# Where the broadcast of the second mixture's first expert stands in a chained attention and mixture kernel

## The chip, the cores and the metric

The kernel runs on one core of a Trainium2 chip. The metric is the device time of one execution in microseconds. Three executions of the kernel before were timed: 648.74 us median, 644.17 the lowest, 648.91 the highest. A further execution was profiled.

## The reference, cut to what matters

Attention over pooled keys and values feeds a first mixture of experts, whose output feeds a second one. Each token goes to one expert; in the second mixture an expert takes at most `capacity` tokens, in token order.

```
x = attention(q, k, v)                     # 2304 tokens, 512 wide
logits = x @ w_gate + modality_bias[modality_id]
e = argmax(logits);  x[mask e] = gate * relu(x[mask e] @ w1[e]) @ w2[e]     # first mixture, 8 experts, F = 1024
logits = x @ w_gate2
e = argmax(logits);  keep the first `capacity` tokens of each expert
out[kept] = gate * relu(x @ w1[e]) @ w2[e]                                    # second mixture
```

## The kernel before, in words

**Tiles and windows.** A mixture is worked in windows of 256 tokens of one expert (two row tiles of 128). In the first mixture window 0 belongs to the first token's expert and has a hand-written order of its own (`first_window`); windows 1 to 9 run through `mixture.body(w, n)`, with n = 2 for a full window and n = 1 for a half one. Which body runs is decided on the chip: every engine reads a flag from a table and branches (L685), so both bodies of each window stand in the program. In the data used, windows 1 to 7 and window 9 are full, and window 8 is the half one.

**The body of a window.** TensorE (PE) computes the first matrix product in four parts, `first(0)` to `first(3)`, and the second product in four parts from them, `second` and `second_ends`. Each float32 value is split in a high and a low part, so each product is three matmuls (L398, L399, L401 and L438, L439, L440). After each `first`, ScalarE (ACT) writes the high part of the hidden tile, `hh` (L405), and VectorE (DVE) the low part, `hl` (L406). Between them stand the transposes of the next window's tokens (L384, with L387 on ACT and L388 on DVE).

**Work on the window before.** While window w is on PE, an object `post1` treats the output of window w - 1: its 16 products with the second gate's columns run on DVE (L747), in groups of 2, 2, 5 and 7 that stand between the parts of the body. Then `gates` finds each token's second expert, `store` sends the rows to memory from GpSimd (POOL, L790), and at the very end of the window `places` puts the experts into the table `e2acc` with two small matmuls (L798) and one DVE addition (L799).

**The guess.** The second mixture starts with the expert of one token, the first row of window 0 of the first mixture. `guess` (L183 to L194) broadcasts that expert number over the partitions with a matmul (L185) and has DVE write seven things from it: the integer `gi` (L186), the rotated order of the experts `rot`, `wrap` (L188 to L191), the table `before2` (L192), the expert as a column `gs` (L193) and its marker `isgs` (L194). In the kernel before this is the end of `places` for token window 0, which is the end of window 1.

**Who reads it.** `gi` is read by the DMA queue of SyncE (SP), in `loads` (L603), where the second mixture's first weights are asked for; `gs` and `isgs` are read in window 8 (`k2.experts`, `k2.others`), `before2` in the second mixture's dispatch.

**Order.** The schedule is written by hand: each engine works through its instructions in the order of the program, and semaphores hold an instruction until what it reads is there. PSUM tiles named "sums" are taken from a pool of two.

Of the kernel before, what the change touches and what calls it, by code (L numbers as in the profile page):

```python
# [6 lines left out]
F32 = mybir.dt.float32  # L7
# [5 lines left out]
ALU = mybir.AluOpType  # L13
# [56 lines left out]
def build(tc, A, out):  # L70
    nc = tc.nc
    V, G, PE, ACT = nc.vector, nc.gpsimd, nc.tensor, nc.scalar
# [7 lines left out]
    def bc(ap, axis, shape):  # L80
        return ap.unsqueeze(axis).to_broadcast(shape)
# [5 lines left out]
    cp = root.enter_context(tc.tile_pool(name="cp", bufs=1))  # L87
# [6 lines left out]
    def C(name, p=128):  # L94
        o, n = _COLS[name]
        return cb[:p, o : o + n]
# [62 lines left out]
    before2 = cp.tile([128, E, E], F32, name="before2")  # L159
# [23 lines left out]
    def guess(psum_ap, ecol, before, slot):  # L183

        mm(psum_ap, C("sel0"), ecol, start=True, stop=True)  # L185
        V.tensor_copy(gi[0:1, slot : slot + 1], psum_ap[0:1, 0:1])  # L186
        rot = cp.tile([128, E], F32, name=f"rot{slot}")
        V.tensor_scalar(rot, iota[:, 0:E], psum_ap, None, ALU.subtract)  # L188
        wrap = cp.tile([128, E], F32, name=f"wrap{slot}")
        V.tensor_scalar(wrap, rot, 0.0, 8.0, ALU.is_lt, ALU.mult)  # L190
        V.tensor_tensor(rot, rot, wrap, ALU.add)  # L191
        V.tensor_tensor(before, bc(rot, 1, [128, E, E]), bc(rot, 2, [128, E, E]), ALU.is_lt)  # L192
        V.tensor_scalar(gs[slot], psum_ap, float(slot), None, ALU.add)  # L193
        V.tensor_scalar(isgs[slot], rot, 0.0, None, ALU.is_equal)  # L194
# [4 lines left out]
    def bank(use, shape):  # L199
        pool, name = banks[use]  # L200
        return pool.tile(shape, F32, name=name)
# [173 lines left out]
    def scatter(ids, k, y, n):  # L375
        for t in range(n):
            G.indirect_dma_start(  # L377
                out[:, :], bass.IndirectOffsetOnAxis(ap=ids[:, k + t : k + t + 1], axis=0),
                y[:, t, 0:DM], None, bounds_check=N - 1, oob_is_err=False)

    def trans(xg, xT, t):
        px = bank("turned", [128, CH, 128])
        for c in range(CH):
            tp(px[:, c, :], xg[t][:, 128 * c : 128 * c + 128], ident)  # L384
        px = px.rearrange("p c (b r) -> p c b r", b=2)
        hi, lo = (xT[:, :, 2 * t : 2 * t + 2, i, :] for i in range(2))
        ACT.copy(hi, px)  # L387
        V.tensor_tensor(lo, px, hi.bitcast(F32), ALU.subtract)  # L388
# [43 lines left out]
    def second(py, hs, q, order=None):  # L432

        for j, t in order or [(j, t) for j in range(2) for t in range(2)]:
            if t < len(hs):
                hh, hl = hs[t]
                st, sp = (q == 0 and j == 0), (q == NF - 1 and j == 1)
                mm(py[t], hh[:, j, :], h2[q][:, j, :], start=st, stop=False)  # L438
                mm(py[t], hh[:, j, :], l2[q][:, j, :], start=False, stop=False)  # L439
                mm(py[t], hl[:, j, :], h2[q][:, j, :], start=False, stop=sp)  # L440

    def second_ends(py, a2, a3):

        second(py, a2, 2, [(0, 0), (1, 0), (0, 1)])
        second(py, a3, 3, [(0, 0), (1, 0)])
        second(py, a2, 2, [(1, 1)])
        second(py, a3, 3, [(0, 1), (1, 1)])
# [96 lines left out]
    class mixture:  # L544
# [69 lines left out]
        def body(self, w, n):  # L614

            m, xT, y = self.m, self.xT(w), self.y(w)
            first = lambda q: (first2 if n == 1 else first4)(xT, q)
            self.gather(w + 2)
            post = post1(w - 1, self.y(w - 1)) if m == 1 else None
            look, found = (m == 1 and w == WK + i for i in range(2))  # L620
            on_pe = n < 2 or look or found

            def products(n):
                if post and not on_pe:
                    post.products(n)

            py = [psy.tile([128, DM], F32, name=f"py{t}") for t in range(n)]
            if look:
                k2.experts()
            products(2)  # L630
            a0 = first(0)
            if look:
                k2.ranks()
            self.split_late(w - 1, 0)
            self.loads(w, 0)
            self.trans(w + 1, 0)
            products(2)
            a1 = first(1)
            if m == 1 and 2 <= w < 8:
                self.clear_out(w - 2)  # L640
            self.split_late(w - 1, 1)
            self.loads(w, 1)
            self.trans(w + 1, 1)
            if look:
                k2.choose()
            products(5)
            second(py, a0, 0)
            a2 = first(2)
            if post and on_pe:
                post.transposes()  # L650
            if look:
                for f in k2.hot(rt):
                    f()
            products(7)
            second(py, a1, 1)
            if found:
                trans(xgk, xTk, 0)
            if post and on_pe:
                post.logits()
                post.gates()  # L660
            if found:
                trans(xgk, xTk, 1)
            a3 = first(3)
            if look:
                k2.fetch()
            self.split_next(w)
            if post and not on_pe:
                post.gates()
            if post:
                post.store()  # L670
            if look:
                k2.others()
            second_ends(py, a2, a3)
            self.scale(y, py, self.xg(w))
            if m == 2:
                scatter(self.d.ids, self.col(w), y, n)
            elif n == 1:
                ACT.copy(y[:, 1, 0:DM], zero[:, 0:DM])
            if post:
                post.places()  # L680
# [23 lines left out]
        def end(self, w):  # L704

            post = post1(w, self.y(w))
            if w == WK:
                for t in range(2):
                    trans(xgk, xTk, t)

            def transposes():
                post.transposes((ACT.copy, ACT.copy))
                split_hi(rr2, h2, range(3, NF))

            split_hi(rr2, h2, range(1), V.tensor_copy)
            split_hi(rr2, h2, range(1, 3))
            split_lo(rr2, h2, l2, V, range(2))
            k2.hs[0] = first4(xTk, 0, k2.room(0), transposes)
            post.logits()
            post.gates()  # L720

            def places():
                post.places()
                V.tensor_tensor(oh2, bc(e2acc, 2, [128, T2, E]), bc(iota[:, 1 : E + 1], 1, [128, T2, E]), ALU.is_equal)
                k2.rest()
                split_lo(rr2, h2, l2, V, range(2, NF))

            k2.hs[1] = first4(xTk, 1, k2.room(1), places)
            post.store()

    class post1:
# [62 lines left out]
        def places(self):  # L794

            pt = bank("sums", [128, T2])
            for t, (op, oi) in enumerate(self.hot):
                mm(pt, op, oi, start=(t == 0), stop=(t == 1))  # L798
            V.tensor_tensor(e2acc, e2acc, pt, ALU.add)  # L799
            if self.w == 0:  # L800
                e0 = wk.tile([128, 1], F32, name="e0")
                V.tensor_scalar(e0, self.ev[:, 0:1], -1.0, None, ALU.add)
                pg = bank("sums", [128, 1])
                guess(pg, e0, before2, 1)

    e1 = cp.tile([128, T1], F32, name="e1")
    oh1 = cp.tile([128, T1, E], BF16, name="oh1")
    e2acc = cp.tile([128, T2], F32, name="e2acc")  # L810
    tok = cp.tile([128, 2 * W], I32, name="tok")
    fixp = cp.tile([128, 2, NT], F32, name="fix")

# [16 lines left out]
    with ExitStack() as es:  # L830
# [377 lines left out]
        for i in range(T1 + 1):  # L1208
# [25 lines left out]
            if i == 10:  # L1234
                early.close()
                wa = root.enter_context(tc.tile_pool(name="wa", bufs=1, side="right", reuse_waits="tile"))
                wk = root.enter_context(tc.tile_pool(name="wk", bufs=2, side="right", reuse_waits="tile"))
# [111 lines left out]
```

## Time and profile before

| | us |
|---|---|
| median of the three timed executions | 648.74 |
| the profiled execution's own time | 646.96 |
| its span, from the first to the last instruction | 645.2 |
| PE busy in it | 589.3 (91%) |
| DVE busy | 409.8 (64%) |
| ACT busy | 226.3 (35%) |
| POOL busy | 149.5 (23%) |

The busy times are of the whole span, which has several stages: attention up to about 130 us, the first mixture from there to about 380 us, the second after that. What one place in the kernel costs is read from a timeline of that place and from tables of short stretches, not from these shares. PE's matmuls overlap, so the distance between the starts of two of them tells what one costs, not its own length.

### The profile page before, as it was taken

Reading aid. Unit: us, or ns where it says so; the run is one execution under the profiler, and the core shown is the slowest. Engines: PE = TensorE matmul, PEld = TensorE weight load, DVE = VectorE, ACT = ScalarE, POOL = GpSimd, SP = SyncE. Lnnn points to the kernel's source line nnn. Section 1 sums busy time; section 2 is a strip of 40 time slices with the busy share of each in tenths; the row PEclk is TensorE's granted clock in tenths of the full one; section 3 lists DMA queues with packets and bytes.
Section 4 is the critical chain, followed back from the end, with each engine's and each line's share of the span. In section 5 each row is a group of like instructions: output and inputs, shape, how many; then the busy total and the mean of one; then the engine's idle time right before and its main releaser. Section 6 shows DMA issues by size and latency. Waiting matters only on the chain. (4 is left out here: it accounts for less than half of the span.)

```text
span 645.2 us, 11898 instructions
## 1 busy us (share of the span) xinstructions
PE 589.3 (91%) x3990; PEld 529.2 (82%) x3990; DVE 409.8 (64%) x1100; ACT 226.3 (35%) x395; POOL 149.5 (23%) x149
## 2 busy tenths in 40 slices
PE   7768898889999999999899889998899999999990
PEld 4658897879899899989888888997789999988980
DVE  4689789697687686786587586227884571228110
ACT  3433674222122212212244432136673362135210
POOL 1197125021112102202213113122221222122200
PEclk7789999799999999999989979999999999999996
DMA  9999696258133023113207403826886763121100
GB/s 244 246 270 235 210 281 214 67 194 301 54 100 117 37 84 118 47 70 117 64 18 228 148 19 107 289 70 205 274 277 214 258 211 127 52 69 43 52 20 23
DMA packets 57683, 93.12 MB, mean 144 GB/s; under 512 B 6345, under 2 KB 31177, under 8 KB 57412
## 3 DMA queue, kind: packets, MB, share of 16 engines
q1 hardware_dynamic: 47764, 63.97, 32.9%
q0 software_dynamic: 7360, 22.77, 11.0%
q10 hardware_dynamic: 2416, 4.74, 1.9%
q8 instruction: 57, 0.93, 0.6%
q14 instruction: 86, 0.70, 0.4%
HBM read 68.22 MB, written 24.89 MB: 144 GB/s over the span
## 5 line engine op out<-in xcount | busy, mean ns | idle before, releaser
L438 PE MATMUL py<-h,hh 128*128 128x512 f32 x296 | 119.2, 403 | 3.3 <-DVE h L205 1.8
L398 PE MATMUL first<-xT,h 128*128 128x256 f32 x480 | 120.4, 283 | 0.8 <-PE sums L185 0.8
L399 PE MATMUL first<-xT,l 128*128 128x256 f32 x480 | 118.7, 280 | 1.1 <-DVE l L209 1.1
L439 PE MATMUL py<-l,hh 128*128 128x512 f32 x296 | 116.4, 393 | 2.2 <-DVE l L209 2.2
L440 PE MATMUL py<-h,hl 128*128 128x512 f32 x296 | 116.6, 394 | 0.0
L405 ACT ACTIVATE hh<-first 128x512 fp32r<-128x512 f32 x64 | 38.2, 598 | 204.2 <-PE first L401 185.8
L406 DVE SCALAR_TENSOR_TENSOR hl<-first,hh 128x512 fp32r<-128x512 f32 x64 | 44.1, 690 | 99.8 <-ACT hh L405 44.7
L399 PEld LDWEIGHTS first<-xT,l 128*128 128x128 f32 x480 | 90.1, 188 | 3.4 <-DVE l L209 1.9
L398 PEld LDWEIGHTS first<-xT,h 128*128 128x128 f32 x480 | 90.1, 188 | 2.4 <-ACT y L612 0.8
L209 DVE TENSOR_TENSOR l<-rr,h 128x1024 fp32r<-128x1024 f32 x72 | 84.4, 1220 | 4.7 <-ACT h L205 4.4
L747 DVE SCALAR_TENSOR_TENSOR junk<-y,wg2b 128x512 bf16<-128x512 f32 x112 | 77.3, 690 | 3.4
L401 PE MATMUL first<-xT,h 128*128 128x256 f32 x480 | 75.9, 279 | 0.0
L438 PEld LDWEIGHTS py<-h,hh 128*128 128x128 f32 x296 | 55.7, 188 | 14.6 <-ACT hh L428 2.6
L440 PEld LDWEIGHTS py<-h,hl 128*128 128x128 f32 x296 | 55.7, 188 | 13.2 <-DVE hl L413 0.6
L439 PEld LDWEIGHTS py<-l,hh 128*128 128x128 f32 x296 | 55.8, 188 | 13.0 <-DVE l L209 3.1
L401 PEld LDWEIGHTS first<-xT,h 128*128 128x128 f32 x480 | 64.9, 188 | 0.0
L205 ACT CAST h<-rr 128x1024 fp32r<-128x1024 f32 x64 | 63.4, 1043 | 4.2 <-issue 4.2
L377 POOL DMA_INDIRECT out<-y,ids x18 | 24.9, 1384 | 159.7 <-ACT y L612 109.5
L790 POOL DMA_INDIRECT ys<-y,tok x20 | 22.1, 1104 | 168.5 <-DVE y L785 105.6
L1028 PE MATMUL pv<-vaug,eT 96*128 96x146 f32 (+1 forms) x240 | 34.7, 320 | 10.2 <-DVE lgh L1041 10.2
L1028 PEld LDWEIGHTS pv<-vaug,eT 96*128 96x128 f32 (+1 forms) x240 | 31.5, 201 | 12.1 <-issue 7.4
L612 ACT ACTIVATE y<-py,xg 128x512 f32<-128x512 f32 x35 | 24.0, 687 | 38.5 <-PE py L440 28.4
(272 smaller groups left out, 884.2 us busy)
## 6 DMA issues: line engine op xcount, KB each, us to landing
rr<-in_moe_w SPq DMA_DIRECT2D x72, 512.0 KB, 5.4
ys<-zero SPq DMA_DIRECT2D x18, 260.0 KB, 4.5
xs<-xt SPq DMA_DIRECT2D x36, 130.0 KB, 2.7
out<-zero ACTq DMA_DIRECT2D x6, 768.0 KB, 4.4
kin<-in_k SPq DMA_DIRECT2D x3, 1024.0 KB, 8.9
vin<-in_v SPq DMA_DIRECT2D x3, 1024.0 KB, 7.8
qin<-in_q SPq DMA_DIRECT2D x4, 512.0 KB, 14.6
wg2b<-wgd SPq DMA_DIRECT2D x1, 2048.0 KB, 7.3
```

Source lines behind the costliest of these rows:

```text
L205: copy(hi[q], raw[q])
L209: eng.tensor_tensor(lo[q], raw[q], hi[q].bitcast(F32), ALU.subtract)
L398: mm(g[:, j, :], h1[q][:, c, fs], hi, start=(c == 0), stop=False)
L399: mm(g[:, j, :], l1[q][:, c, fs], hi, start=False, stop=False)
L401: mm(g[:, j, :], h1[q][:, c, fs], xT[:, c, :, 1, :], start=False, stop=(c == CH - 1))
L405: ACT.activation(hh, g, AF.Relu)
L406: V.scalar_tensor_tensor(hl, g, 0.0, hh.bitcast(F32), ALU.max, ALU.subtract)
L438: mm(py[t], hh[:, j, :], h2[q][:, j, :], start=st, stop=False)
L439: mm(py[t], hh[:, j, :], l2[q][:, j, :], start=False, stop=False)
L440: mm(py[t], hl[:, j, :], h2[q][:, j, :], start=False, stop=sp)
L747: V.scalar_tensor_tensor(junk, self.y[:, t, 0:DM], 1.0, wg2b[:, e, :], ALU.mult, ALU.mult, accum_out=self.lg[:, t, e : e + 1])
L1028: mm(pv[p0 : p0 + n, j : j + 2, :], eT[:, 3 * half + j, p0 : p0 + n], vaug[b][:, half, j], start=(j == 0), stop=(j == 2), skip_group_check ...
```

## The change

`e20`, the expert number as a column, becomes a tile of its own that stays for the whole kernel, and is still computed by DVE at the end of window 1. The call of `guess` leaves `places` and stands in `body` for window 2, behind `first(0)` and ahead of `split_late`, in both bodies (full and half). Nothing of what `guess` computes is changed, and the number of instructions is the same.

```
             products(2)
             a0 = first(0)
+            if m == 1 and w == 2:
+                guess(bank("sums", [128, 1]), e20, before2, 1)
             if look:
                 k2.ranks()
             self.split_late(w - 1, 0)
...
             V.tensor_tensor(e2acc, e2acc, pt, ALU.add)
             if self.w == 0:
-                e0 = wk.tile([128, 1], F32, name="e0")
-                V.tensor_scalar(e0, self.ev[:, 0:1], -1.0, None, ALU.add)
-                pg = bank("sums", [128, 1])
-                guess(pg, e0, before2, 1)
+                V.tensor_scalar(e20, self.ev[:, 0:1], -1.0, None, ALU.add)
...
     e2acc = cp.tile([128, T2], F32, name="e2acc")
+    e20 = cp.tile([128, 1], F32, name="e20")
```

## Rows read from the trace of the kernel before

**Rows 1.** Table of stretches, windows 1 to 3: length, busy (count) by engine, PEclk.
```profile
151.00:174.70 23.70, 22.52 (x146) 20.05 (x144) 17.98 (x58) 5.16 (x9) 1.42 (x2) 1.00 0.54 190
174.70:198.30 23.60, 23.57 (x154) 21.26 (x155) 17.72 (x55) 4.47 (x8) 3.98 (x4) 1.00 0.22 72
198.30:221.66 23.36, 23.36 (x157) 21.17 (x157) 17.51 (x53) 5.16 (x9) 4.27 (x4) 1.00 0.24 83
```
**Rows 2.** Timeline, PE and DVE, window 1 to 2: start us, length, instruction, idle before.
```profile
172.69 0.39 PE L440 MATMUL py<-h,hl 128*128 128x512 f32 x1
...
172.93 0.21 PE L798 MATMUL sums<-oi,op 128*128 128x18 bf16 x2
...
173.26 0.17 DVE L799 TENSOR_TENSOR e2acc<-e2acc,sums 128x18 f32<-128x18 f32 x1 [2.06 <-PE sums L798]
173.35 0.15 DVE L802 TENSOR_SCALAR e<-ev 128x1 f32<-128x1 f32 x1
...
173.55 0.38 PE L185 MATMUL sums<-e,cb 128*128 128x1 f32 x2 [0.42 <-DVE e L802]
173.97 0.15 DVE L186 CAST gi<-sums 1x1 int32<-1x1 f32 x1 [0.47 <-PE sums L185]
...
174.73 0.35 PE L398 MATMUL first<-xT,h 128*128 128x256 f32 x1 [0.79 <-PE sums L185]
...
174.92 0.16 DVE L194 TENSOR_SCALAR isg<-rot 128x8 f32<-128x8 f32 x1
...
176.13 0.63 DVE L739 TENSOR_SCALAR op<-cb,tkf 128x128 bf16<-128x128 f32 x2 [1.05 <-issue]
```
**Rows 3.** Timeline of PE from window 2 to 3.
```profile
198.01 0.39 PE L440 MATMUL py<-h,hl 128*128 128x512 f32 x1
...
198.25 0.21 PE L798 MATMUL sums<-oi,op 128*128 128x18 bf16 x2
...
198.31 0.37 PE L398 MATMUL first<-xT,h 128*128 128x256 f32 x1
```
**Rows 4.** Timeline of PE where the half window 8 begins.
```profile
316.37 0.72 PE L422 MATMUL first<-xT,h 128*128 128x256 f32 x4 [1.16 <-ACT y L612]
```
**Rows 5.** Timeline of PE in window 2: one group of transposes, the matmul after it.
```profile
177.73 0.60 PE L384 MATMUL turned<-cb,xg 128*128 128x128 f32 x4
...
178.09 0.36 PE L398 MATMUL first<-xT,h 128*128 128x256 f32 x1
```
**Rows 6.** Timeline of DVE in window 2: the four writes of hl.
```profile
178.64 0.69 DVE L406 SCALAR_TENSOR_TENSOR hl<-first,hh 128x512 fp32r<-128x512 f32 x1 [0.62 <-ACTq L577]
...
181.88 0.69 DVE L406 SCALAR_TENSOR_TENSOR hl<-first,hh 128x512 fp32r<-128x512 f32 x1 [0.36 <-ACT hh L405]
...
187.85 0.69 DVE L406 SCALAR_TENSOR_TENSOR hl<-first,hh 128x512 fp32r<-128x512 f32 x1 [0.90 <-ACT hh L405]
...
193.48 0.69 DVE L406 SCALAR_TENSOR_TENSOR hl<-first,hh 128x512 fp32r<-128x512 f32 x1
```
**Rows 7.** Timeline of PE in window 2: the first matmul that reads the last hl.
```profile
195.21 0.40 PE L440 MATMUL py<-h,hl 128*128 128x512 f32 x1
```
**Rows 8.** Timeline of POOL and DVE in window 2: the two gathers, a product beside.
```profile
177.22 0.99 POOL L373 DMA_INDIRECT xg<-xs,rows  x1 [0.51 <-issue]
...
177.32 0.69 DVE L747 SCALAR_TENSOR_TENSOR junk<-y,wg2b 128x512 bf16<-128x512 f32 x1
...
178.51 0.98 POOL L373 DMA_INDIRECT xg<-xs,rows  x1 [0.30 <-DMA ys<-y,tok]
```
**Rows 9.** Timeline in attention: the first mixture's own guess, POOL beside it.
```profile
62.01 2.37 POOL L892 TENSOR_TENSOR tree<-vin 128x1024 f32<-128x1024 f32 x1 [2.10 <-DMA vin<-in_v]
...
62.15 2.26 DVE L194 TENSOR_SCALAR isg<-rot 128x8 f32<-128x8 f32 x1
```
**Rows 10.** SP's queue, line 603: its read of gi (count, ns, start us).
```profile
L603 SPq TENSOR_LOAD <-gi x1: 267/267/267, 216.5 to 216.5; - x1
```
**Rows 11.** Waits of SP's queue: who for whom, us in total, times, longest.
```profile
SPq L106 <- DVE l L209: 120.3, 1, 120.3
```

More of the change, by code (lines that the diff above doesn't have):

```diff
@@ L631, in body @@
             a0 = first(0)
+            if m == 1 and w == 2:
+                guess(bank("sums", [128, 1]), e20, before2, 1)
             if look:
@@ L800, in places @@
             if self.w == 0:
[L801 to L804, printed above, removed]
+                V.tensor_scalar(e20, self.ev[:, 0:1], -1.0, None, ALU.add)
     e1 = cp.tile([128, T1], F32, name="e1")
@@ L810, in build @@
     e2acc = cp.tile([128, T2], F32, name="e2acc")
+    e20 = cp.tile([128, 1], F32, name="e20")
     tok = cp.tile([128, 2 * W], I32, name="tok")
```

## The prediction

> **What bounds the kernel.** I read the table of stretches first, window by window through the first mixture, to learn which engine sets the pace there. In window 3 PE is busy for all of its 23.36 us and DVE for 17.51 [rows 1]; windows 4 to 7 repeat that within 0.1 us. So a full window lasts as long as PE's matmuls, and an idle stretch of PE around it is paid in full. Windows 1 and 2 are the two that are longer, 23.70 and 23.60 us [rows 1]. [...]
>
> Second, I read the timeline of PE and DVE across the border of windows 1 and 2 [rows 2]. The reader is to see a chain that passes from engine to engine: the last matmul of the window starts at 172.69, the two of `places` at 172.93, DVE adds them at 173.26, then computes the expert number at 173.35, and only then can PE do the broadcast, at 173.55, after 0.42 us of idling for it. The next window's first matmul starts at 174.73, with 0.79 us idle before it. From the last L440 to that L398 it is 174.73 - 172.69 = 2.04 us. Third, the same distance at the next border: 198.31 - 198.01 = 0.30 us [rows 3]. The borders of windows 3 to 4, 4 to 5, 5 to 6, 6 to 7 and 8 to 9 show 0.30 as well, so six in all; only the entry into the half window 8 is longer.
>
> The page's chain that ended last is of no help here: it follows the second mixture's scatters and never comes to this place.
>
> **The change part by part.**
>
> *The broadcast leaves the border.* If window 1 then ends like the other full ones, the border goes from 2.04 to 0.30: 1.74 us won on PE. The 0.42 us are surely tied to the broadcast, which waits for DVE. The 0.79 us behind it need a reading: the row puts them down to the broadcast itself [rows 2], though that had ended at 173.93, and no data that `first(0)` reads was late. I take it that PE's queue runs ahead over the branch while matmuls are still at work, and can't when its next matmul waits for DVE. At the other six borders, which have the same branch and no such wait, L398 follows L798 by 0.06 us [rows 3]. So I count the 0.79 as won too. The bounds are 1.74 - 0.79 = 0.95 and, if window 2's surplus over window 3 also goes (23.60 - 23.36 = 0.24 [rows 1]), 1.74 + 0.24 = 1.98 us.
>
> *The broadcast enters window 2 on PE.* Two matmuls with their weight loads, between `first(0)` and the transposes. Four transposes, as short as these, take 178.09 - 177.73 = 0.36 us from their start to the next one's [rows 5], 0.09 each, so two take 0.18; the broadcast's own 0.38 us for both [rows 2] is the upper end, if nothing overlaps. I take 0.23, near the transposes, which load weights of the same 128 columns and move more data. Its wait is free: in the new place PE comes to it 177.73 - 174.73 = 3.0 us after the window's first matmul [rows 2, 5], about 176.0, and `e20` is written at about 173.5 (173.35 + 0.15 [rows 2]). Its PSUM tile is free too, since the addition that last read one ends at 173.43.
>
> *The seven DVE instructions enter window 2.* From 173.97 to 174.92 + 0.16 = 175.08 they take 1.11 us [rows 2]. At the border they lay beside PE's idling; DVE's next work, L739, started 1.05 us after them. Now they stand behind the first write of `hl` and ahead of the low half of the transposed tokens (L388). Queued behind them on DVE are that L388, two products, and the second `hl`. DVE idles for 0.36 us ahead of the second `hl` and 0.90 us ahead of the third, both times for ACT, which waits for PE [rows 6]: 1.26 us, more than 1.11. So the third `hl` is written when it was, and the fourth, ahead of which DVE doesn't idle, as well. If this cover were gone, the next to feel it would be the fourth `hl`: it ends at 193.48 + 0.69 = 194.17 [rows 6] and the matmul that first reads it starts at 195.21 [rows 7], 1.04 us to spare. The second `hl`, up to 0.75 us late, is read only after `first(2)`, several us on. I cost this at nothing; the bounds are 0 and 1.11 us.
>
> *e20 instead of e0, gi later.* One DVE instruction as before, in the same place: nothing. `gi` comes some 4 us later than at 174.1. SP's queue is the one that reads it, at 216.5 [rows 10], and behind that it stands for 120.3 us, until DVE has used up the old weights [rows 11]. The other readers come in window 8. Nothing is late; POOL has no instruction in the guess, and its stores and gathers are issued in the same order.
>
> *Sum.* 1.74 - 0.23 = 1.51 us less. Against the profiled execution's own 646.96 that is 645.45. That execution lies 1.78 under the median of the three timed, from which the sum gives 647.23. As 644.17 to 648.91 is shown for one kernel, neither anchor is better; I put the time midway, at 646.3. A move of 1% either way (6.5 us) is about what a measurement of this kernel can tell from no change, and every case here lies within it.
>
> **The rivals.**
>
> *The branch keeps its price.* The 0.79 us could belong to the branch into window 2 and not to the broadcast. For it: the entry into the half window shows 1.16 us of idling where no data was awaited that another border lacks [rows 4]. Against it: six borders without such a pause, with the same branch to the full body. Gain 0.95 - 0.23 = 0.72: 646.2 by the profiled execution, 648.0 by the median. [...]
>
> *The gain is given back.* Something later that doesn't move with PE would take up the 1.5 us, and the time stays at 647.0 (648.7 by the median). For it: the page's chain runs through DMA and issue. Against it: the only large load of weights that is asked for ahead of its turn is held by DVE's use of the old ones [rows 11], so it moves with the windows.
>
> *DVE is held by POOL, and slower.* The same marker instruction L194 took 2.26 us in attention, where POOL's addition ran from 62.01 to 64.38 beside it [rows 9], against 0.16 at the border. In its new place the guess falls on POOL's gathers, 0.99 and 0.98 us long [rows 8]. If DVE's work there grows by more than 1.26 + 1.04 = 2.30 us, PE waits at the fourth `hl`; from 2.30 + 1.51 = 3.81 us on, the change is slower than before. Two instructions held like that one would make 1.11 + 2 x 2.10 = 5.31, so a stall of 3.0 and 1.5 us more than before: 648.5, or 650.2 by the median. Against it: the gathers are shorter than that addition, and a product that runs beside one takes its usual 0.69 [rows 8]; even held for both gathers, 1.11 + 1.97 = 3.08, the change would still gain 0.7. [...]
>
> **How the numbers follow.** The forecast, a gain between 1.2 and 1.9 us, gets 0.78; the branch that keeps its price 0.09; the gain given back 0.09; slower by DVE 0.04. All four lie within 3.0 us of each other, less than the 4.7 us between the timed executions, so the range is made of that spread: from 644.17 less 1.5, 642.7, to 648.91, which is where the gain given back would still put the highest, so 649.0. Faster by over 1% would need under 642.3: 0.04, for a lucky set of executions. Slower by over 1%: 0.02. Within: 0.94.
>
> **What would show it.** Right: from the last L440 of window 1 to the first L398 of window 2 some 0.3 us; L185 in window 2 with no idling before it; seven DVE instructions of together 1.1 us behind the first `hl`; the idle times of 0.36 and 0.90 us ahead of the second and third `hl` smaller or gone; the fourth `hl` over 1 us ahead of its reader; window 2 about 0.2 us longer on PE, and all later borders 1.5 us earlier. Wrong: a pause of 0.8 us that stays at the border; L194 or its neighbours over 1 us beside a gather; PE idling in window 2; or a later wait of PE grown by what the border lost.

## The result, and the profile after

The changed kernel takes 652.57 us (median of 20 executions), the kernel before 648.12 beside it: a ratio of 1.0097, with a 95% interval of 1.007 to 1.0124. The ratio is taken over fast executions alone (one of the changed kernel's 20 is left out) and is not the quotient of the two medians, which is 1.0069. It is slower, where a gain of 1.5 us was forecast, and 652.57 lies above the forecast's range of 642.7 to 649.0. The profiled execution took 648.68 us with a span of 646.9.

At the place of the change the trace shows what was forecast. First the timeline of PE and DVE from window 1 to 2, which answers to [rows 2].

```profile
173.24 0.39 PE L440 MATMUL py<-h,hl 128*128 128x512 f32 x1
173.48 0.21 PE L800 MATMUL sums<-oi,op 128*128 128x18 bf16 x2
173.54 0.36 PE L398 MATMUL first<-xT,h 128*128 128x256 f32 x1
...
173.91 0.15 DVE L803 TENSOR_SCALAR e<-ev 128x1 f32<-128x1 f32 x1
...
176.50 0.28 PE L185 MATMUL sums<-e,cb 128*128 128x1 f32 x2
...
176.64 0.63 PE L384 MATMUL turned<-cb,xg 128*128 128x128 f32 x4
```

The border takes 173.54 - 173.24 = 0.30 us, not 2.04, and the broadcast waits for nothing: `e20` is written 2.4 us ahead of it. Then DVE and POOL in window 2, and PE's first read of the last `hl` (they answer to [rows 6 to 8]).

```profile
177.52 0.69 DVE L406 SCALAR_TENSOR_TENSOR hl<-first,hh 128x512 fp32r<-128x512 f32 x1
177.99 0.99 POOL L373 DMA_INDIRECT xg<-xs,rows  x1 [0.33 <-issue]
178.13 0.14 DVE L186 CAST gi<-sums 1x1 int32<-1x1 f32 x1
...
178.44 0.17 DVE L190 TENSOR_SCALAR wrap<-rot 128x8 f32<-128x8 f32 x1
...
179.06 0.16 DVE L194 TENSOR_SCALAR isg<-rot 128x8 f32<-128x8 f32 x1
...
181.32 0.68 DVE L406 SCALAR_TENSOR_TENSOR hl<-first,hh 128x512 fp32r<-128x512 f32 x1
...
186.93 0.69 DVE L406 SCALAR_TENSOR_TENSOR hl<-first,hh 128x512 fp32r<-128x512 f32 x1 [0.54 <-ACT hh L405]
...
192.58 0.69 DVE L406 SCALAR_TENSOR_TENSOR hl<-first,hh 128x512 fp32r<-128x512 f32 x1
...
194.32 0.40 PE L440 MATMUL py<-h,hl 128*128 128x512 f32 x1
```

The seven instructions run from 178.13 to 179.22, 1.09 us, beside a gather (177.99 to 178.98), and none is stretched: 0.14 to 0.23 us each, 0.15 to 0.22 before. L194, which took 2.26 us beside POOL's addition in attention, takes 0.16 here, but starts 0.08 us after the gather's end; L190, an instruction of the same kind and size, runs inside it and takes its usual 0.17 us. DVE's idle times ahead of the second and third `hl` shrink from 0.36 and 0.90 to 0 and 0.54, and the fourth `hl` ends at 193.27, still 1.05 us ahead of its reader. SP reads `gi` at 217.0, and its longest wait is the same (120.6 us, for L209).

The loss is in windows that hold nothing of the change. The table of stretches for windows 2 to 4 (columns as in [rows 1]):

```profile
173.54:197.42 23.88, 23.88 (x160) 21.52 (x159) 18.35 (x61) 5.17 (x9) 4.21 (x5) 1.00 0.26 82
197.42:221.11 23.69, 23.69 (x157) 21.32 (x157) 17.57 (x53) 5.17 (x9) 4.28 (x4) 1.00 0.26 82
221.11:244.81 23.70, 23.70 (x158) 21.33 (x157) 17.57 (x53) 5.17 (x9) 4.36 (x4) 1.00 0.24 80
```

Window 3 takes 23.69 us and not 23.36, and windows 4 to 6 take 23.70. PE has no idle time in them, as many instructions (157 or 158 in a stretch) and the same granted clock of 1.00: it does the same work in 1.4% more time. The page's costliest groups say which work; first the kernel before, then the changed one (count, busy us, mean ns of one).

```profile
L398 PE MATMUL first<-xT,h 128*128 128x256 f32 x480 | 120.4, 283 | 0.8 <-PE sums L185 0.8
L399 PE MATMUL first<-xT,l 128*128 128x256 f32 x480 | 118.7, 280 | 1.1 <-DVE l L209 1.1
L439 PE MATMUL py<-l,hh 128*128 128x512 f32 x296 | 116.4, 393 | 2.2 <-DVE l L209 2.2
```

```profile
L398 PE MATMUL first<-xT,h 128*128 128x256 f32 x480 | 121.9, 286 | 0.0
L399 PE MATMUL first<-xT,l 128*128 128x256 f32 x480 | 120.2, 282 | 1.2 <-DVE l L209 1.2
L439 PE MATMUL py<-l,hh 128*128 128x512 f32 x296 | 117.3, 396 | 2.2 <-DVE l L209 2.2
```

These matmuls are 2 to 3 ns longer in the mean. Their steps tell it better, that is the distance between the starts of two neighbours, averaged over windows 3 to 6: in the first product (367 distances) 119.26 ns before and 121.31 after, in the second (176) 229.48 and 233.03. (The first product's means hold seven distances of some 200 ns, each the first behind other work; without them they are 117.64 and 119.73, and this 117.64 is the 117.7 of two expectations below.) Over the kernel's 3 x 480 matmuls of the first and 3 x 296 of the second that makes 1440 x 2.05 + 888 x 3.55 = 6.1 us. That takes windows 3 to 6 for the whole kernel and is too much: averaged over the whole kernel, distances over 180 and 300 ns left out, the steps go from 117.68 to 119.44 and from 230.61 to 233.03, which makes 1440 x 1.76 + 888 x 2.42 = 4.7 us.

What has changed for these matmuls is where their operands lie. The built programs give their SBUF tiles addresses from both ends: the "left side" from the low addresses upwards (an added tile of 4 bytes puts `xT0` 32 bytes up, e1 below), the "right side" from the high ones downwards (a tile added there puts `h1_0` 32 bytes down, e4). In the allocation of both programs, all tiles stand at multiples of 32 bytes; `e20` moves every later tile on the left side by 32 bytes, and the absence of `e0` moves `hh` and `hl` by 64. In bytes, modulo 128 in brackets: `h1_0` 184224 (32) in both; `xT0` 104416 (96) before, 104448 (0) after; `hh` 172000 (96) and 172064 (32); `h2_0` 59168 (32) and 59200 (64).

### The profile page after: what moved, and what is told of

Read it like the earlier page. It is cut to its first block, busy times and chain, and to the rows that moved or that the text cites. A ratio compares the mean times of both kernels' runs of the same rounds, so it can differ in the third digit from the quotient of the medians.

```text
span 646.9 us, 11898 instructions
## 1 busy us (share of the span) xinstructions
PE 594.1 (92%) x3990; PEld 530.2 (82%) x3990; DVE 411.9 (64%) x1100; ACT 226.7 (35%) x395; POOL 149.1 (23%) x149
## 5 line engine op out<-in xcount | busy, mean ns | idle before, releaser
L398 PE MATMUL first<-xT,h 128*128 128x256 f32 x480 | 121.9, 286 | 0.0
L399 PE MATMUL first<-xT,l 128*128 128x256 f32 x480 | 120.2, 282 | 1.2 <-DVE l L209 1.2
L440 PE MATMUL py<-h,hl 128*128 128x512 f32 x296 | 116.9, 395 | 0.0
L209 DVE TENSOR_TENSOR l<-rr,h 128x1024 fp32r<-128x1024 f32 x72 | 84.4, 1221 | 4.6 <-ACT h L205 4.4
L401 PE MATMUL first<-xT,h 128*128 128x256 f32 x480 | 77.0, 282 | 0.0
L440 PEld LDWEIGHTS py<-h,hl 128*128 128x128 f32 x296 | 55.5, 187 | 13.8 <-DVE hl L413 0.8
L1028 PE MATMUL pv<-vaug,eT 96*128 96x146 f32 (+1 forms) x240 | 33.1, 307 | 10.9 <-DVE lgh L1041 10.9
L1028 PEld LDWEIGHTS pv<-vaug,eT 96*128 96x128 f32 (+1 forms) x240 | 29.8, 191 | 12.7 <-issue 6.3
```

The source lines that it names most:

```text
L209: eng.tensor_tensor(lo[q], raw[q], hi[q].bitcast(F32), ALU.subtract)
L398: mm(g[:, j, :], h1[q][:, c, fs], hi, start=(c == 0), stop=False)
L399: mm(g[:, j, :], l1[q][:, c, fs], hi, start=False, stop=False)
L401: mm(g[:, j, :], h1[q][:, c, fs], xT[:, c, :, 1, :], start=False, stop=(c == CH - 1))
L1028: mm(pv[p0 : p0 + n, j : j + 2, :], eT[:, 3 * half + j, p0 : p0 + n], vaug[b][:, half, j], start=(j == 0), stop=(j == 2), skip_group_check ...
```

## The experiments

**Theory:** the addresses lengthen PE's steps, wherever the guess stands. **Rival:** the moved code does. The table has the operands' places modulo 128 (of the first product h1 and xT, of the second hh and h2), the steps in ns, the length of window 3 in us, the measured ratio with its interval, and a ratio by estimate. The estimate takes each step's difference to the kernel before, times 1440 and 888, and 0.8 us less where the guess is moved (from e2, below), over 648. As it goes by windows 3 to 6, it tends to be high: with the steps of the whole kernel the change comes to 1.006, e1 and e4 to 1.008.

| run | guess | h1, xT | first | hh, h2 | second | window 3 | ratio | estimate |
|---|---|---|---|---|---|---|---|---|
| before | old | 32, 96 | 119.26 | 96, 32 | 229.48 | 23.36 | | |
| after | moved | 32, 0 | 121.31 | 32, 64 | 233.03 | 23.69 | 1.0097 (1.007 to 1.0124) | 1.008 |
| e5, the same again | moved | 32, 0 | 121.31 | 32, 64 | 233.03 | 23.70 | 1.0068 (1.0032 to 1.0105) | 1.008 |
| e1 pad only | old | 32, 0 | 121.25 | 96, 64 | 233.68 | 23.71 | 1.0052 (1.0026 to 1.0078) | 1.010 |
| e2 move only | moved | 32, 96 | 119.27 | 96, 32 | 229.49 | 23.35 | 0.9986 (0.9958 to 1.0014) | 0.999 |
| e14, e2 again | moved | 32, 96 | 119.26 | 96, 32 | 229.48 | 23.35 | 0.9981 (0.9952 to 1.0009) | 0.999 |
| e3 after, 64 bytes | moved | 32, 32 | 120.10 | 32, 96 | 231.66 | 23.56 | 1.0018 (0.9984 to 1.0052) | 1.004 |
| e4 right pad | old | 0, 96 | 121.29 | 64, 32 | 233.59 | 23.73 | 1.0072 (1.0045 to 1.01) | 1.010 |
| e6 after, right pad | moved | 0, 0 | 120.08 | 0, 64 | 232.49 | 23.58 | 1.0036 (0.9996 to 1.0075) | 1.005 |
| e7 xT alone | old | 32, 0 | 121.27 | 96, 32 | 229.52 | 23.52 | 1.0067 (1.0029 to 1.0106) | 1.004 |
| e8 hh alone | old | 32, 96 | 119.40 | 64, 32 | 233.24 | 23.53 | 1.0105 (1.0046 to 1.0164), 6 executions | 1.005 |
| e9 hh at 32 | moved | 32, 96 | 119.46 | 32, 32 | 228.62 | 23.31 | 0.9976 (0.994 to 1.0013) | 0.998 |
| e10 all at 64 | moved | 0, 64 | 116.43 | 64, 0 | 233.02 | 23.24 | 0.995 (0.9919 to 0.998) | 0.997 |
| e11 left 96 | moved | 32, 64 | 120.00 | 96, 0 | 233.91 | 23.62 | one execution, 648.90 us | 1.006 |
| e12 left 64 | moved | 32, 32 | 120.07 | 96, 96 | 232.68 | 23.56 | one execution, 651.74 us | 1.005 |
| e13 best pairs | moved | 0, 64 | 116.78 | 32, 32 | 232.80 | 23.24 | 0.9957 (0.9924 to 0.999) | 0.998 |

**e1: the pad without the move.**

```
     e2acc = cp.tile([128, T2], F32, name="e2acc")
+    pad = cp.tile([128, 1], F32, name="pad")
```

> The guess stays at the end of window 1; only a tile of 4 bytes that nobody uses is added behind e2acc, which moves every tile behind it on the left side of SBUF by 32 bytes (xT0 from 104416 to 104448, h2_0 from 59168 to 59200), while h1 (184224) and hh (172000) stay. Theory of the addresses (the new tile e20 slows PE by where it puts the operands): windows 3 to 7 take 23.6 to 23.7 us each and not 23.36, the border of windows 1 to 2 keeps its 2.04 us, the time is 1.0 to 1.4% above the kernel before. Rival, the moved code itself makes PE's later windows longer: windows of 23.36 us and a ratio of 1.000 within 0.3%.

**e2: the move without the pad.**

```
-    cap = cp.tile([128, 1], F32, name="cap")
+    cape = cp.tile([128, 2], F32, name="cap")
+    cap, e20 = cape[:, 0:1], cape[:, 1:2]
...
             if self.w == 0:
+                e0 = wk.tile([128, 1], F32, name="e0")
                 V.tensor_scalar(e20, self.ev[:, 0:1], -1.0, None, ALU.add)
```

> The guess is moved as in the change, but e20 lies in a spare column of the tile cap and the tile e0 is still allocated, so that every tile has the address of the kernel before. Theory of the addresses: windows 3 to 7 take 23.36 us, the border of windows 1 to 2 takes 0.30 us, the ratio is 0.997 to 0.999 (1.5 us less). Rival, the moved code: windows of 23.6 to 23.7 us and a ratio of about 1.01.

Windows 3 and 4 of e1:

```profile
199.65:223.36 23.71, 23.71 (x158) 21.34 (x157) 17.57 (x53) 5.16 (x9) 4.29 (x4) 1.00 0.24 82
223.36:247.07 23.71, 23.71 (x157) 21.34 (x157) 17.58 (x53) 5.17 (x9) 4.30 (x4) 1.00 0.24 80
```

and of e2, with window 2 ahead:

```profile
175.03:198.70 23.67, 23.67 (x160) 21.38 (x159) 18.65 (x61) 5.16 (x9) 4.26 (x5) 1.00 0.26 83
198.70:222.05 23.35, 23.35 (x157) 21.16 (x157) 17.56 (x53) 5.16 (x9) 4.05 (x4) 1.00 0.25 83
222.05:245.41 23.36, 23.36 (x158) 21.16 (x157) 17.52 (x53) 5.16 (x9) 4.33 (x4) 1.00 0.25 81
```

This settles the main question. A tile of 4 bytes that nobody reads makes the windows as long as the change does, with the guess in its old place; the moved guess at the old addresses leaves them as they were. The rival falls. e1's ratio of 1.0052, with an interval up to 1.0078, is below the 1.010 expected; its windows are not.

**e3 and e4: other distances.** e3 makes `e20` 64 bytes wide; e4 takes the kernel before and adds a tile on the right side.

```
-    e20 = cp.tile([128, 1], F32, name="e20")
+    e20 = cp.tile([128, 16], F32, name="e20")[:, 0:1]
```

```
                 xTk = wa.tile([128, CH, 4, 2, 64], F32R, name="xT_k")
+                pad = wa.tile([128, 1], F32, name="pad")
```

> The changed kernel, with e20 64 bytes wide, so that the left side moves by 64 bytes and not by 32; e0 is gone, so hh and hl lie 64 bytes higher as in the changed kernel. Theory of the addresses, if what counts is the address modulo 64 (xT0 at 104480, 32 modulo 64 as before): windows of 23.36 us and a ratio of 0.997 to 0.999. If what counts is the address modulo 128 or the distance between operands: windows of 23.6 us, ratio about 1.01. Rival, the moved code: windows of 23.6 to 23.7 us, ratio about 1.01; it is told from the modulo 128 case by e2.

> The guess stays as before and the left side too; a tile of 4 bytes on the right side moves h1, l1, hh and hl by 32 bytes down (h1_0 from 184224 to 184192, 0 modulo 64; xT0 stays at 104416, 32 modulo 64). If the place of the weights and of the moving operand relative to each other counts, this is as slow as the changed kernel: windows of 23.6 us, ratio 1.01. If only the left side's own place counts: windows of 23.36 us, ratio 1.000. If weights at a multiple of 64 are read faster: windows below 23.3 us, ratio below 0.998.

e4 moves only the operands on the right side (h1, l1, hh and hl, which PE's LDWEIGHTS take, 128x128 each) and is as slow as the change: it isn't the left side by itself. e3 comes out between the two, so neither "modulo 64" nor "modulo 128" as I had them.

**e5 and e6: the change again, and the change with e4's tile.** e5 is the changed kernel, e6 has the second edit of above on top of it.

> The changed kernel itself, beside the three others of this group on one chip. Both theories: windows 3 to 7 of 23.69 us, as in its first profile, and a ratio of 1.006 to 1.012. It is the measure for e6.

> The changed kernel with one more tile of 4 bytes on the right side: h1, l1, hh and hl move by 32 bytes, so that now the left side (xT0 at 104448, h2_0 at 59200) and the right side (h1_0 at 184192, hh at 172032) lie at multiples of 64. If the distance of weights and moving operand modulo 64 counts: windows of 23.35 us, the border of windows 1 to 2 0.30 us, a ratio of 0.996 to 0.999. If an operand at a multiple of 64 is itself slow: windows of 23.7 us or more, ratio 1.01 or above.

e5 gives the same steps as the first profile, to a hundredth of a nanosecond, in another execution: they belong to the program. One of e5's 12 executions took 1153.75 us and isn't in its ratio; the cause is not known. e6 takes back 0.11 us of the 0.33 per window; the distance modulo 64 isn't the rule.

**e7 and e8: one operand each, in the kernel before.**

```
+    pads = [wsp.tile([128, 1], F32, name="pad0")]
     xTs = [wsp.tile([128, CH, 4, 2, 64], F32R, name=f"xT{i}") for i in range(2)]
+    pads.append(wsp.tile([128, 1], F32, name="pad1"))
```

```
                 e0 = wk.tile([128, 1], F32, name="e0")
+                pad = wk.tile([128, 1], F32, name="pad", bufs=1)
```

> The kernel before, with pads of 32 bytes ahead of and behind the two tiles xT: xT0 goes from 104416 to 104448, all that lies behind them moves by 64, h2, l2, h1 and hh stay. If the distance of the two operands of one matmul counts: L398, L399 and L401 start every 119.5 to 120.5 ns and not every 117.7, L438 to L440 every 230 as before, windows of 23.55 to 23.6 us, ratio 1.004. If the place of the whole left side counts (through DVE's or ACT's reads): no change of L398 alone, windows of 23.35 or all steps longer.

> The kernel before, with hh and hl 32 bytes lower (172000 to 171968), while h1, h2 and xT stay. If the distance of the two operands of one matmul counts: L438 to L440 start every 233 to 234 ns and not every 230, L398 to L401 every 117.7 as before, windows of 23.48 to 23.55 us, ratio 1.003. Otherwise: windows of 23.35 us, ratio 1.000.

Groups of PE in e7, then in e8:

```profile
L398 PE MATMUL first<-xT,h 128*128 128x256 f32 x480 | 121.9, 285 | 0.9 <-PE sums L185 0.9
L439 PE MATMUL py<-l,hh 128*128 128x512 f32 x296 | 116.5, 394 | 2.2 <-DVE l L209 2.2
```

```profile
L398 PE MATMUL first<-xT,h 128*128 128x256 f32 x480 | 120.4, 283 | 0.9 <-PE sums L185 0.9
L439 PE MATMUL py<-l,hh 128*128 128x512 f32 x296 | 117.0, 395 | 2.2 <-DVE l L209 2.2
```

Each product feels its own operand: with `xT` moved only the first is slower, with `hh` moved only the second (by the steps 2.0 and 3.8 ns). So the place matters through the product that reads the tile, not through a whole side.

A rival is left: DVE, ACT, POOL and DMA use the moved tiles too and could get in PE's way. The traces of before and after settle it. In windows 3 to 6, distances over 180 ns left out, the first product's step is 117.64 ns before and 119.73 after. Over those steps beside which none of the three engines ran it is 117.80 (20 steps) and 120.00 (14), and over those without a DMA packet under way 117.69 (198) and 119.90 (189). For the second product, beside an idle DVE, it is 229.97 (32) and 232.89 (37). The lengthening is there without the others, so it isn't theirs.

**e9 to e12: more pairs.** All are e2 with other places: e9 without the unused `e0`; e11 and e12 with a pad of 96 and 64 bytes behind `e2acc`; e10 as e11 with e4's tile too.

```
     e2acc = cp.tile([128, T2], F32, name="e2acc")
+    pad = cp.tile([128, 24], F32, name="pad")
```

> The kernel of e2 without the unused tile e0: hh and hl lie 64 bytes higher (172064, 32 modulo 128), and h2 stays (59168, 32 modulo 128), so the two operands of the second product are 0 apart modulo 128 and not 64; h1 and xT stay. Theory of the addresses: L398 to L401 keep their mean step of 119.3 ns; L438 to L440 go from 229.5 to 231 to 233 ns, windows of 23.41 to 23.55 us, ratio 1.000 to 1.003. Rival, only multiples of 64 against 32 modulo 64 count: no change against e2, 23.35 us, 0.998.

> The kernel of e2 with the left side 96 bytes higher and the right side 32 lower: h1 at 0, xT at 64, hh at 64, h2 at 0 modulo 128, so both products have their operands 64 apart, as in the kernel before, but all at multiples of 64. If the distance alone counts: windows of 23.35 us, steps of 119.3 and 229.5 ns, ratio 0.997 to 0.999. If the place modulo 64 counts too: other steps at the same distance, windows of 23.45 us or more.

> The kernel of e2 with the left side 96 bytes higher alone: first product's operands 32 apart modulo 128 (h1 32, xT 64), second's 96 before (hh 96, h2 0, so 32 apart round the end). Theory of the addresses: both products slow, means of about 121.3 and 233 to 234 ns, windows of 23.69 to 23.72 us. Rival, only the one place of 32 bytes of the change is bad: windows of 23.35 us.

> The kernel of e2 with the left side 64 bytes higher: both products have their operands at the same place modulo 128 (h1 and xT 32, hh and h2 96). Theory of the addresses: the first product as in e3 and e6, 120.1 ns; the second between 229.5 and 232.5 ns; windows of 23.42 to 23.58 us. Rival, any distance that is a multiple of 64 is equal: windows of 23.35 us.

e9's second product gets 0.9 ns shorter, against the expectation. e11 misses too: its first product steps every 120.00 ns, not 121.3, and its window 3 takes 23.62 us, not 23.69 or more. e12 comes out as expected but for the second product, 232.68 and not at most 232.5. e10 is faster than both kernels: its first product steps every 116.43 ns, 2.8 less than before, though its second is slow. Windows 3 and 4 of e10:

```profile
197.86:221.10 23.24, 23.24 (x157) 20.88 (x157) 17.52 (x53) 5.17 (x9) 4.63 (x4) 1.00 0.25 83
221.10:244.35 23.25, 23.25 (x158) 20.89 (x157) 17.53 (x53) 5.16 (x9) 4.05 (x4) 1.00 0.24 82
```

**e13 and e14: the best pairs together, and e2 again.** e13 is e2 with e4's tile, e8's tile, 96 bytes ahead of `xTs` and 32 behind.

> The guess moved as in e2, with the places of the shortest steps so far, modulo 128: h1 at 0 and xT at 64 (as in e10, 116.4 ns against 119.3), hh at 32 and h2 at 32 (as in e9, 228.6 ns against 229.5). Theory of the addresses: windows of 23.0 to 23.1 us; over the kernel some 1440 matmuls of the first product 2.8 ns shorter (4.1 us) and about 890 of the second 0.9 ns shorter (0.8 us), with the move's own gain of 0.8 to 1.6 us a ratio of 0.989 to 0.992. If the steps of the two products hang on each other or on DVE's reads: windows of 23.2 us or more and a ratio above 0.994.

> The same kernel as e2. The move alone, at equal addresses: 1.65 us less at the border and in window 2, some 0.7 to 1.5 us given back where the half window begins, so 0.1 to 1.0 us less in all, a ratio of 0.9985 to 1.000. Rival, the 1.5 us of the prediction hold: 0.9975 to 0.998.

e13 is a miss: the first product keeps nearly its short step, but the second doesn't have e9's 228.62 with the same places modulo 128 (there `hh` is at 172064, here at 171936). So the places modulo 128 of one product's operands don't fix its step. It still beats both kernels, like e10, but with 0.9957 and not the 0.989 to 0.992 expected. e14 has e2's steps again; its interval holds both the ratio that it expected and that of its rival.

**The half window.** At the entry of window 8 the moved kernels lose time. PE's two branches there (L685, in the changed kernel L687) with the count, the least, median and longest in ns; first before, then after:

```profile
L685 PEldq COMPARE_BRANCH  x2: 375/1481/2587, 312.8 to 313.6; - x2
```

```profile
L687 PEldq COMPARE_BRANCH  x2: 1027/1820/2613, 313.5 to 315.0; - x2
...
317.77 0.71 PE L422 MATMUL first<-xT,h 128*128 128x256 f32 x4 [1.72 <-issue]
```

The first branch takes 371 to 380 ns in the five kernels with the guess in its old place and 1027 to 1417 in the eleven profiles with it moved (means 0.38 and 1.23 us). From the last L440 to the first L422 it is 1.50 to 1.97 us in the five (mean 1.77) and 2.16 to 3.11 in the eleven (mean 2.61). So the move costs some 0.84 us there, as much as the first branch grew by. Two DMA queues of the traces, q8 and q14, are of the kind "instruction", and q8 has packets of 16384 bytes that fall in with PE's branches. This is its line on the page, the same before and after:

```profile
q8 instruction: 57, 0.93, 0.6%
```

In all eleven a packet of it lands between 0.36 us ahead of the first branch's start and 0.02 us behind it, and the branch ends 1.37 to 1.40 us after that landing. In the five the last packet had landed 1.99 to 2.35 us ahead of the branch. The second branch, 2.59 to 3.13 us in all sixteen, has a packet of its own that starts 0.26 to 0.30 us after it. So the branch is longer where the packet lands later. That it waits for this packet is my reading of these times; no view names what holds it. The late packet comes with the moved code: e2, with the old addresses, has it, and the pads without the move (e1, e4, e7, e8) don't. How the move delays the packet isn't shown.

## Why the prediction was wrong, point by point

- **The broadcast leaves the border:** right. 0.30 us in the changed kernel, and the pause of 0.79 us went with the wait, so the branch did not keep its price there. The reading behind it is in the traces as well. In the kernel before, PE's queue comes to the branch 1.18 us ahead of the window's first matmul, just when the broadcast is released. It then takes 0.32 us for one branch, 0.47 for the read of a flag and 0.07 for a second branch. In the changed kernel it comes there 2.41 us ahead, while matmuls are still queued. The queue of instruction packets that falls in with PE's branches (q8, see the half window) starts none in the pause until 0.12 us before its end, so all but the end of the pause lies beside no packet of that queue.
- **The broadcast enters window 2 on PE:** right. In e2 it is 0.14 us from the broadcast's start to that of the transposes, and the transposes take 0.39 us to the next matmul's start and not 0.36: 0.17 us; 0.23 was taken. (Window 2 against window 3 doesn't give this price: it was 0.23 us longer before the broadcast stood in it, 23.58 against 23.35.) At the old addresses border and window 2 together go from 2.04 + 23.58 = 25.62 (from the starts of the first matmuls) to 0.30 + 23.67 = 23.97 in e2: 1.65 us won, 1.51 forecast.
- **The seven DVE instructions:** right, at no cost. They lie beside a gather and take 1.09 us, so this gather did not hold DVE.
- **e20 instead of e0:** this is the step that failed. It was put as "One DVE instruction as before, in the same place: nothing". The instruction is the same, but the tile isn't: its 32 bytes, and the 64 that `e0` leaves free, move operands of both products. By the steps that costs 4.7 to 6.1 us; e1 shows `e20`'s part alone, and e2 the move without either. All four cases of the forecast looked at instructions and waits, so none held this one; the chance of 0.02 for a loss of over 1% came from that. That the loss, 0.97%, stays just inside the 1% that got 0.94 is luck.
- **Nothing given back later:** wrong in part, 0.84 us at the half window. With it the move alone is worth 1.65 - 0.84 = 0.8 us, 0.999. e2 and e14 measure 0.9986 and 0.9981, both with intervals that include a ratio of 1, so that small a gain isn't shown by time, only by the traces.
- **The sum:** 6.1 - 0.8 = 5.3 us more, a ratio of 1.008, or 4.7 - 0.8 = 3.9 and 1.006 by the steps of the whole kernel; 1.0097 and 1.0068 were measured. The lower estimate lies in the second's interval and just below the first's, 1.007 to 1.0124. The two profiled executions differ by just 1.72 us, less than executions of one kernel do (641.40 to 651.37 for the kernel before); the windows' lengths, not the two totals, carried the reading.

Open: what in the addresses makes a matmul's step. Shown is only that it hangs on the places of the operands, product by product. A single place doesn't fix it (`xT` at 0 gives 121.3 with `h1` at 32 and 120.1 with `h1` at 0), nor does the distance (hh and h2 64 apart give 229.5, 231.7, 232.5 and 233.0).

## What to carry to other kernels

Count a new or removed tile as a change of every operand behind it: compare the allocated addresses of the operands of the busiest engine before and after, and where they moved, compare the steps of untouched stretches first. A control with the same addresses (a spare column of an existing tile, an unused tile kept) separates an edit from its layout. Where an engine runs without idle time, trying a few places for its operands is an experiment of its own: here only e10 and e13, the edit with other places, are clear of the kernel before on the fast side; the edit alone (e2) isn't.

## What the runs showed of the hardware that was not expected

- Shifts of 32 to 96 bytes in the operands' SBUF addresses move the step of a float32r matmul between 116.4 and 121.3 ns (256 columns) and between 228.6 and 233.9 ns (512 columns), at a granted clock of 1.00; the steps repeat to 0.01 ns in other executions (the changed kernel and e5, e2 and e14).
- The best layout tried (e10, with the guess moved) is 0.5% faster than the kernel before (0.9919 to 0.998), the change as made 1.0% slower.
- One and the same branch of PE took 0.38 us or 1.0 to 1.4 us, with the broadcast's four PE instructions (two weight loads, two matmuls) in one window or in the next. The longer one ended 1.37 to 1.40 us after an instruction packet of 16384 bytes (q8) had landed, in all eleven profiles that have it.
